# Half of the second plain expert as a fourth kind of group, and token sums of two batches made during attention

## The chip, the cores and the metric

The kernel runs on one core of one Trainium2 chip. The time is device microseconds of that core: 1470.93 us, the median of three runs (1470.7 to 1470.96).

## The reference

A gated linear attention is followed by a mixture of experts.

```
state = 0                                   # per batch (4) and head (8): 48 x 48
for t in range(768):
    state = f[t, :, None] * state + outer(k[t], v[t])      # f = sigmoid(f_logit)
    y[t] = q[t] @ state
x = y as (3072 tokens, 384 features)
P = exp(x @ w_gate - max)                   # 3072 x 8
8 times: P /= P.sum(1) + 1e-9; P /= P.sum(0) + 1e-9; P *= 3072 / 8
out = sum over e in 0..7 of P[:, e] * (relu(x @ w1[e]) @ w2[e])     # 384 -> 1024 -> 384
```

Every expert sees every token, so nearly all of the work is dense products.

## The kernel before

Each number is held as two fp16 parts (h and l), and a product is made of three: hh, hl, lh. The tokens are cut into 4 batches of 768; a batch is two units `u` of 384 tokens, a unit three tiles `t` of 128. The 1024 features of an expert are 8 tiles `f` of 128.

The program has three stages on the one core.

**Attention with plain experts as its filler.** There are 24 attention items, one for each 128 tokens. An item loads `q3` (decay, q, k) and `vr`, runs two scans on VectorE, makes fp16 parts on ScalarE and GpSimd, transposes by a DMA, and gives TensorE 24 products `aps`, 24 `kvps`, 48 `yps`, and 6 of the gate (`lps`). Its result is written into `xh` and `xl`, the two parts of the tokens. The code of an item is a generator. A loop over steps `g` advances each item that is alive by one `yield`; an item begins every 8 steps (`STEPS`), the fourth at step `LEADS`. In each step `fill(n)` adds so many TensorE products of the plain experts as the table `FILL` says for that step. The plain experts are 0 and 1 for all 8 units (`RAW`, 16 pairs of expert and unit): for a unit, 72 products `hps` (x by w1), then 72 `yps` (h by w2), all with 384 columns. The first three units (`TILED`) are done in tiles of 128 tokens, with `hps` products of 128 columns. After each `hps` bank ScalarE writes `hh`, the relu in fp16, and VectorE `hl`, what fp16 left out. A result `yr` goes to DRAM (`ys`) and is read back and scaled much later (`readds`).

**The balance.** After the last item the gate numbers `lg` of all tokens go through `sinkhorn`: eight rounds of small VectorE operations with one product `sk_c` each, which end in `pes`, the weight of each token and expert. Plain products go on as filler, 8 for a step. Beside them `convert` turns the tokens of a batch into the 15 sums that the third stage needs: `x32` (h + l), 17 sums `xs` on GpSimd, three maxima `xmx` on VectorE, then two fp16 parts of each (`xah`, `xal`, `xbh`, `xbl`), which take the place of `xh` and `xl`, so they come when no plain expert reads these tokens any more.

**Groups.** 48 groups (`ORDER`), one for each expert 2 to 7, half of its features (`m`, 512) and batch. A group makes the products with fewer multiplications: 15 block products for 18 with w1 (90 products of 256 columns), 7 for 8 with w2 in three blocks (126 products of 192 columns). The weights of a group are prepared some groups ahead (`prepare_w1`, `prepare_w2`). Before the first group, five products `kb_touch` mark the hand-over of the PSUM banks.

The order on each engine is fixed: `pin` chains each instruction behind the one before it on its engine, and `mm` does so on TensorE. Where the chain is cut (`last.clear()` before the groups), the scheduler may place an instruction earlier.

Of the kernel before, what the change touches and what calls it, by code (L numbers as in the profile page):

```python
# [50 lines left out]
RAW = [(e, u) for u in range(5) for e in range(2)] + [(0, 5), (0, 6), (0, 7), (1, 5), (1, 6), (1, 7)]  # L51
# [227 lines left out]
def fast(ctx, tc, qkf, vbd, wg, w1, w2, out, flag):  # L279
# [44 lines left out]
    psa = pctx.enter_context(tc.tile_pool(name="psa", bufs=2, space=PSUM))  # L324
# [60 lines left out]
    banks = [0]  # L385

    def bank(shape, name):
        n = banks[0]
        banks[0] += 1
        return (psn if n % 2 and not late else psm).tile(shape, F32, name=name, tag="m")  # L390

    def moe(e, u, w):
        w1s, w2s = w
# [3 lines left out]
        hh, hl = [], []  # L397
        for f in range(FT):
# [10 lines left out]
            th, tl = (hp.tile([128, 2, 256], F16, name=f"h{q}_{e}_{u}_{f}", tag=f"k{q}{f // 6}{f % 6 // 3}{f % 3}").rearrange("p c t -> p (c t)")[:, 0:HS] for q in "hl")  # L409
# [5 lines left out]
            yield 1  # L415
        for t in range(TT):
            ts = slice(t * 128, t * 128 + 128)
            ps = bank([128, DM], f"yps_{e}_{u}_{t}")
            n = 0
            for f in range(FT):  # L420
                wh, wl = w2s[f // 2]
                for a, b in ((hh[f], wh), (hh[f], wl), (hl[f], wh)):
                    mm(out=ps, lhsT=a[:, ts], rhs=b[:, f % 2, :], start=(n == 0), stop=(n == 3 * FT - 1))
                    n += 1
                    if n < 3 * FT:
                        yield 1
            with at(EPRIO):
                yr = rp.tile([128, DM], F32, name=f"yr_{e}_{u}_{t}", tag="yraw", bufs=3)
                pin(nc.scalar.activation(out=yr, in_=ps, func=AF.Copy))
                nc.sync.dma_start(out=yscr[e][u, t * 128:(t + 1) * 128], in_=yr)  # L430
            yield 1

    tiles, put_off, owed = [0], [False], []

    def moe_tile(e, u, t):
        w1s, w2s = ws[e]
# [4 lines left out]
        h = []  # L441
        for g in range(2):
# [24 lines left out]
            h.append([v.rearrange("p (f t) -> p f t", t=128) for v in (th, tl)])  # L467
            yield 1 / 3
        ps = bank([128, DM], f"yps_{e}_{u}_{t}")
        n = 0  # L470
        for f in range(FT):
            if len(owed) > 1 - f // 4:
                raise RuntimeError("a low part is owed")
            wh, wl = w2s[f // 2]
            hh, hl = (v[:, f % 4, :] for v in h[f // 4])
            for a, b in ((hh, wh), (hh, wl), (hl, wh)):
                mm(out=ps, lhsT=a, rhs=b[:, f % 2, :], start=(n == 0), stop=(n == 3 * FT - 1))
                n += 1
                if n < 3 * FT:
# [3 lines left out]
        nc.sync.dma_start(out=yscr[e][u, t * 128:(t + 1) * 128], in_=yr)  # L483
        yield 1
# [34 lines left out]
    def gate(i, xh, xl, tok):  # L519
        ps = psa.tile([128, 2 * NE], F32, name=f"lps{i}", tag="a", bufs=1)  # L520
# [18 lines left out]
    def early_item(i):  # L539
# [21 lines left out]
        r = ap.tile([R, L], F32, name=f"r_{i}", tag="r")  # L561
# [18 lines left out]
        qh = ap.tile([R, L], F16, name=f"qh_{i}", tag="qh")  # L580
        ql = ap.tile([R, L], F16, name=f"ql_{i}", tag="ql")
# [42 lines left out]
        aps = psa.tile([128, NB, C], F32, name=f"aps_{i}", tag="a", bufs=1)  # L624
# [23 lines left out]
        if i:  # L648
            kept = ap.tile([R, NP, D], F32, name=f"u1_{i}", tag="u1")
# [21 lines left out]
        yps = psa.tile([128, NP, TS], F32, name=f"yps_{i}", tag="y", bufs=1)  # L671
# [32 lines left out]
    def item(i):  # L704
# [15 lines left out]
        r = ap.tile([R, L], F32, name=f"r_{i}", tag="r")  # L720
# [21 lines left out]
        qh = ap.tile([R, L], F16, name=f"qh_{i}", tag="qh")  # L742
        ql = ap.tile([R, L], F16, name=f"ql_{i}", tag="ql")
# [10 lines left out]
        yield from wait(4)  # L754
# [7 lines left out]
        aps = psa.tile([128, NB, C], F32, name=f"aps_{i}", tag="a", bufs=1)  # L762
# [774 lines left out]
```

## Time and profile before

| | |
|---|---|
| median of three runs | 1470.93 us |
| the profiled execution | 1472.75 us |
| its span, first to last instruction | 1471.0 us |
| TensorE, share of the span with a matmul under way | 98% |
| VectorE / ScalarE / GpSimd busy | 82% / 74% / 72% |
| granted TensorE clock, mean | 0.995 |

The profile is of one execution; the difference of 1.75 us between its time and its span lies outside the instructions. An instruction that is still under way counts as busy, also while the next one of its engine has begun; so the busy time of a stretch is less than the sum of the durations in it. In the 40 slices of the page a digit is a busy share in tenths.

### The profile page before, as it was taken

The numbers are of one execution on the slowest core, as the hardware profiler recorded it, in microseconds if no ns is written. First come the engines' busy times: TensorE is split into PE (matmuls) and PEld (weight loads), VectorE is DVE, ScalarE is ACT, GpSimd is POOL, SyncE is SP. The second block draws the span as 40 slices with busy tenths as digits, with TensorE's granted clock in tenths as the row PEclk, the third lists the DMA queues.
The fourth block names the chain that finished last, engine by engine and source line by source line (L and its number), as shares of the span: only waits on it lengthen the run. The fifth ranks groups of instructions, "written<-read, shape, count | busy, mean of one in ns | idle before, by whom it ended". The sixth has DMA issues, their size and how long they took to land.

```text
span 1471.0 us, 40358 instructions
## 1 busy us (share of the span) xinstructions
PE 1445.4 (98%) x16051; PEld 1258.1 (86%) x16051; DVE 1208.6 (82%) x2494; ACT 1085.2 (74%) x2428; POOL 1062.2 (72%) x1242
## 2 busy tenths in 40 slices
PE   7899999999999999999999999999999999999997
PEld 5688886666666799999999999999999999999996
DVE  8767677775685799889998988888898989888776
ACT  7767777774343777888888888888877777778764
POOL 3244544555458566999999999999998888888763
PEclk9999999999999999999999999999999999999999
DMA  8345445441001101222111111111111101000012
GB/s 263 110 114 123 111 125 127 122 109 41 17 33 39 44 13 29 61 62 62 55 53 54 54 55 40 50 50 55 49 34 34 34 26 31 13 21 14 2 55 79
DMA packets 82807, 90.51 MB, mean 62 GB/s; under 512 B 49872, under 2 KB 69456, under 8 KB 82608
## 3 DMA queue, kind: packets, MB, share of 16 engines
q1 hardware_dynamic: 82176, 87.25, 21.3%
q8 instruction: 127, 2.08, 0.6%
q14 instruction: 72, 0.59, 0.1%
q10 hardware_dynamic: 432, 0.59, 0.1%
HBM read 64.03 MB, written 14.16 MB: 53 GB/s over the span
## 4 chain that ended last, share of the span: by engine, by line
PE 90%; DVE 5%; ACT 3%; DMA 1%; issue 1%; POOL 0%; DVEq 0%; ACTq 0%
PE kyps L307 28%; PE yps L307 14%; PE hps L307 11%; PE kb_A L307 8%; PE kb_B L307 8%; PE kb_D L307 6%; PE kxps L307 5%; PE kb_C L307 4%; PE kb_E L307 2%; PE kb_F L307 2%; PE aps L307 1%; PE kvps L307 1%; DMA w1r<-in_w_dram 0%; DVE w2l L380 0%; DVE acc L1242 0%
## 5 line engine op out<-in xcount | busy, mean ns | idle before, releaser
L307 PEld LDWEIGHTS <-k1h 128*128 128x128 f16 x2880 | 270.9, 98 | 22.4 <-issue 3.5
L307 PE MATMUL kyps<-k2h,kgh 128*128 128x192 f16 x1152 | 283.4, 246 | 1.5 <-ACT kyps L1239 1.5
L307 PE MATMUL kyps<-k2l,kgh 128*128 128x192 f16 x1152 | 283.4, 246 | 0.0
L307 PE MATMUL kyps<-k2h,kgl 128*128 128x192 f16 x1152 | 283.4, 246 | 0.0
L307 PEld LDWEIGHTS <-kgh 128*128 128x128 f16 x2304 | 212.1, 98 | 8.2 <-issue 1.8
L1412 POOL TENSOR_TENSOR kgl<-kf,kgh 128x512 f16<-128x512 f32 x141 | 186.7, 1324 | 2.8 <-ACT kgh L1409 2.8
L1242 DVE SCALAR_TENSOR_TENSOR yy<-kyps,pes,part 128x192 f32<-128x192 f32 x258 | 106.9, 415 | 89.8 <-PE kyps L307 78.9
L1412 POOL TENSOR_TENSOR kgl<-kr,kgh 128x512 f16<-128x512 f32 x141 | 167.2, 1186 | 9.5 <-PE kyps L307 8.1
L1281 POOL TENSOR_TENSOR acc<-acc,yy 128x384 f32<-128x384 f32 x129 | 129.1, 1001 | 61.4 <-DVE yy L1242 61.4
L307 PEld LDWEIGHTS <-k1l 128*128 128x128 f16 x1440 | 140.9, 98 | 16.3
L307 PE MATMUL yps<-w2h,hh 128*128 128x384 f16 x384 | 126.6, 330 | 1.9 <-ACT hh L458 1.8
L307 PE MATMUL yps<-w2h,hl 128*128 128x384 f16 x384 | 126.5, 329 | 1.2 <-DVE hl L461 1.2
L307 PE MATMUL yps<-w2l,hh 128*128 128x384 f16 x384 | 126.5, 329 | 0.4 <-DVE w2l L380 0.3
L307 PEld LDWEIGHTS <-w1h 128*128 128x128 f16 x1344 | 97.3, 98 | 33.4 <-issue 2.1
L307 PEld LDWEIGHTS <-hh 128*128 128x128 f16 x768 | 74.7, 99 | 47.8 <-ACT hh L458 2.4
L307 PEld LDWEIGHTS <-kh 128*128 128x128 f16 x1152 | 108.2, 98 | 8.1 <-issue 1.8
L307 PEld LDWEIGHTS <-kgl 128*128 128x128 f16 x1152 | 112.7, 98 | 0.2 <-issue 0.2
L1363 ACT ACTIVATE cp<-kb_A 128x512 f32<-128x512 f32 x144 | 86.1, 598 | 20.0 <-DVE kb_A L1365 16.3
L1239 ACT ACTIVATE kyps<-kyps 128x192 f32<-128x192 f32 x144 | 46.3, 322 | 66.0 <-PE kyps L307 63.3
L1409 ACT ACTIVATE kgh<-kf 128x512 f16<-128x512 f32 x144 | 91.0, 632 | 0.9 <-DVE kf L1386 0.6
L1409 ACT ACTIVATE kgh<-kr 128x512 f16<-128x512 f32 x144 | 90.4, 628 | 0.0
L1389 POOL TENSOR_TENSOR kr<-kr 128x256 f32<-128x256 f32 x96 | 72.9, 759 | 22.1 <-ACT kr L1378 20.1
(310 smaller groups left out, 5282.0 us busy)
## 6 DMA issues: line engine op xcount, KB each, us to landing
q<-in_qkf_dram SPq DMA_DIRECT2D x23, 672.0 KB, 5.3
k1r<-in_w_dram SPq DMA_DIRECT2D x24, 384.0 KB, 3.0
ys<-yr SPq DMA_DIRECT2D x48, 192.0 KB, 2.2
k2r<-in_w_dram SPq DMA_DIRECT2D x24, 384.0 KB, 3.1
yb<-ys SPq DMA_DIRECT2D x48, 192.0 KB, 2.4
vr<-in_vbd_dram SPq DMA_DIRECT2D x24, 192.0 KB, 2.5
out_dram<-acc SPq DMA_DIRECT2D x21, 192.0 KB, 1.9
w1r<-in_w_dram SPq DMA_DIRECT2D x8, 384.0 KB, 8.7
```

What stands on the lines that cost most here:

```text
L307: ins = (nc.tensor.transpose if transpose else nc.tensor.matmul)(**kw)
L1239: pin(nc.scalar.activation(out=out, in_=in_, func=AF.Copy, **kw))
L1242: pin(nc.vector.scalar_tensor_tensor(out=y, in0=ps, scalar=p, in1=z, op0=ALU.mult, op1=ALU.add))
L1281: pin(nc.gpsimd.tensor_tensor(out=y, in0=y, in1=z.rearrange("p s d -> p (s d)"), op=ALU.add))
L1363: pin(nc.scalar.activation(out=fresh(ev[2]), in_=bk, func=AF.Copy))
L1389: pin((nc.gpsimd if ev[2] == 'P' else nc.vector).tensor_tensor(out=r[:, 0], in0=r[:, 1], in1=r[:, 0], op=ALU.subtract))
L1409: pin(nc.scalar.activation(out=hs['g', t][0][i], in_=hs['f' if i else 'r', t], func=AF.Copy))
L1412: pin((nc.vector if tag == str(PERIODS - 1) else nc.gpsimd).tensor_tensor(out=hs['g', t][1][i], in0=hs['f' if i else 'r', t], in1=hs['g', ...
```

## The change

1. `FEATS` gives expert 1 only its first 4 feature tiles as a plain expert. Its other 512 features become four groups, (1, 1, b) for the four batches, at the head of `ORDER`, which now has 52 groups. Expert 1 loads four plain weight tiles for eight.
2. `RAW` goes through the pairs by unit; only the last pair is left over to the end of the filler (`RAW_END`), before three were.
3. Plain pairs are cut in an up part (w1) and a down part (w2), and the up part of what comes next is put ahead of a down part: always for the tiles, and one feature tile of the next pair for expert 1.
4. The converts of batches 0 and 1 run during attention (`EARLY`: from step 60 and from step 150, one `yield` in four steps). The other two begin at steps 1 and 30 of the balance, before at 26 and 50 (and the last at 67); the first group weights at step 13, before 34.
5. `LEADS` is 17 for 23, and `FILL` drops from 8.7, 8.1 a step to 5.6, 6.4 and 6.9.
6. An attention item has nine more waits (`MIDDLE` 6, `LATER` 2, one `yield`); the gate comes 6 steps behind x, before 4. From item 6 on, the fourth block of the tokens is written as one 96 x 128 piece `x3` on ScalarE and one on VectorE (before, three 32 x 128 pieces on each), and six DMAs on SP's queue move them to their partitions.
7. Some buffers of an item go from two to one, `qh` and `ql` to three, and the two `kvps` of an item share one PSUM bank, of which there is one (before two).
8. Tables of due steps for the weights of the groups (`W1AT0`, `W2AT0`, `W2AT1`, `W2AT3`, `CONVAT`) and for the plain weights of expert 1 (`SECONDAT`) are written anew.

Counted in the program: 324 `hps` products of 128 columns, 180 of 384, and 288 `yps` of 384 go away; 4 x 216 products of groups are added. 108 DMAs of x3 are added.

```diff
-RAW = [(e, u) for u in range(5) for e in range(2)] + [(0, 5), (0, 6), (0, 7), (1, 5), (1, 6), (1, 7)]
+FEATS = (FT, FT // 2)
+RAW = [(e, u) for u in range(3) for e in range(2)] + [(0, 3), (1, 3), (0, 4), (1, 4), (0, 5), (1, 5), (0, 6), (1, 6), (0, 7), (1, 7)]
+RAW_END = 1
...
-ORDER = [(e, m, b) for e in range(2, NE) for m in range(2) for b in range(B)]
+ORDER = [(e, m, b) for e in range(1, NE) for m in range(2) if (e, m) != (1, 0) for b in range(B)]
...
-LEADS = 23
-FILL = (... (17, 5.3), (23, 8.7), (30, 8.7), (43, 8.1), (48, 8.1))
+LEADS = 17
+FILL = (... (17, 5.3), (23, 5.6), (48, 6.4), (112, 6.9), (160, 6.9))
...
-CONVSTEP = (26, 50, 67)
-KSTEP = 34
+CONVSTEP = (1, 30)
+KSTEP = 13
+EARLY = ((60, 4, 30), (150, 4, 13))
...
+        if i >= X3_FROM:
+            x3 = ap.tile([96, 2, TS], F16, name=f"x3_{i}", tag="x3", bufs=1)
+            pin(nc.scalar.activation(out=x3[:, 0, :], in_=yps[0:96, 3], func=AF.Copy, scale=YS * XS))
...
+            pin(nc.vector.scalar_tensor_tensor(out=x3[:, 1, :], in0=yps[0:96, 3], scalar=YS * XS, in1=x3[:, 0, :], op0=ALU.mult, op1=ALU.subtract))
...
+            for q, x in enumerate((xh, xl)):
+                for n in range(3):
+                    nc.sync.dma_start(out=x[96:128, n, tok], in_=x3[32 * n:32 * n + 32, q, :])
...
+        for e, u, t in todo:
+            h = []
+            yield from tile_up(e, u, t, h)
+            behind_.append((e, u, t, h))
+            while len(behind_) > (0 if e == u == 0 and t < TT - 1 or (e, u, t) == (1, 0, TT - 1) or u and e else 1):
+                yield from tile_down(*behind_.pop(0))
...
+            yield from moe_up(*p, h)
+            if p[0] and n + 1 < len(todo):
+                first_up[todo[n + 1]] = ([], [])
+                yield from moe_up(*todo[n + 1], first_up[todo[n + 1]], 1)
+            yield from moe_down(*p, h)
...
+        for b, (begin_, every, most) in enumerate(EARLY):
+            if begin_ <= g < begin_ + every * most and (g - begin_) % every == 0:
+                next(converts[b], None)
```

Two places in the order of VectorE bear on the prediction. The first is in the first 70 us. `w2l` is the low part of a plain weight tile, `k2r` the raw tile of weights of the first group, whose transfer can begin only when `w2l` has freed a buffer; `wmx` reads it. Before:

```order
L380 SCALAR_TENSOR_TENSOR w2l_2_1163<-w2r_2_709,w2h_2_1162 128x768
L732 SCALAR_TENSOR_TENSOR q_3_1019<-q_3_1019,r_1129 112x512
L733 SCALAR_TENSOR_TENSOR vlc_1134<-vr_1021,vhc_1133 128x384
L734 SCALAR_TENSOR_TENSOR q_3_1019<-ft_129,pi_130 112x512
L380 SCALAR_TENSOR_TENSOR w2l_3_1167<-w2r_3_725,w2h_3_1166 128x768
L1096 TENSOR_REDUCE wmx<-k2r_0_8525 128x1
L461 SCALAR_TENSOR_TENSOR hl_0_0_0_1250<-hps_0_0_0_1211,hh_0_0_0_1249 128x512
```

And now:

```order
L397 SCALAR_TENSOR_TENSOR w2l_3_556<-w2r_3_186,w2h_3_555 128x768
L640 TENSOR_TENSOR carry_715<-kvps_586,st_576 112x192
L601 SCALAR_TENSOR_TENSOR q_2_494<-ft_129,pi_130 112x512
L723 SCALAR_TENSOR_TENSOR xl_318<-yps_641,xh_317 96x3x128
L723 SCALAR_TENSOR_TENSOR xl_318<-yps_641,xh_317 32x128 x3
L607 TENSOR_TENSOR q_2_494<-q_2_494 112x512
L555 TENSOR_REDUCE lg<-lps_732 128x8
L647 TENSOR_TENSOR kb_128<-q_2_494,kb_128 48x8x64 x2
L1158 TENSOR_REDUCE wmx<-k2r_2_7605 128x1
L661 SCALAR_TENSOR_TENSOR vlc_748<-vr_496,vhc_747 128x384
```

`wmx` stood straight behind the `w2l` that frees the buffer; now nine instructions stand between, and it is one item earlier.

The second place is the end of the balance, ahead of `kb_A`, the first VectorE work of the groups. Before, these rows stand ahead of it, and `pes` 36 rows ahead:

```order
L412 SCALAR_TENSOR_TENSOR hl_7_5_8385<-hps_7_5_8370,hh_7_5_8384 128x384
L1024 TENSOR_REDUCE xmx<-x_3_8296 128x1
L412 SCALAR_TENSOR_TENSOR hl_7_6_8402<-hps_7_6_8388,hh_7_6_8401 128x384
L412 SCALAR_TENSOR_TENSOR hl_7_7_8420<-hps_7_7_8405,hh_7_7_8419 128x384
L1024 TENSOR_REDUCE xmx<-x_3_8296 128x1
L1365 TENSOR_TENSOR kb_A<-kb_A,cp_13_8552 128x512
```

And now:

```order
L168 TENSOR_SCALAR sk_cs<-sk_c_7520 128x8
L169 RECIPROCAL sk_cs<-sk_cs 128x8
L170 TENSOR_SCALAR sk_cs<-sk_cs 128x8
L172 TENSOR_TENSOR pe<-pe,sk_cs 128x192
L1113 TENSOR_SCALAR pes<-pe 128x192
L1418 TENSOR_TENSOR kb_A<-kb_A,cp_13_7624 128x512
```

The last round of the balance now stands directly ahead of the groups. On TensorE, 396 products stand between the last gate product and the first `kb_touch`, before 682.

## Rows read from the trace of the kernel before

**Rows 1.** The page: busy time of each engine, and the chain of work that ended last by engine.

```profile
PE 1445.4 (98%) x16051; PEld 1258.1 (86%) x16051; DVE 1208.6 (82%) x2494; ACT 1085.2 (74%) x2428; POOL 1062.2 (72%) x1242
...
PE 90%; DVE 5%; ACT 3%; DMA 1%; issue 1%; POOL 0%; DVEq 0%; ACTq 0%
```

**Rows 2.** Busy time by stretch (start:end, length, then busy us and count of each engine, granted clock, DMA share, GB/s). The stretches are cut where items 1, 2, 3, 6 and 22 give TensorE their `yps`, and by the stages.

```profile
33.59:50.94 17.35, 15.01 (x225) 11.45 (x222) 14.63 (x25) 11.45 (x23) 4.02 (x6) 1.00 0.45 137
50.94:89.05 38.11, 35.56 (x492) 28.25 (x490) 25.55 (x43) 25.64 (x51) 12.83 (x13) 0.96 0.43 113
89.05:130.81 41.76, 41.45 (x700) 34.36 (x698) 29.75 (x58) 29.95 (x65) 19.52 (x20) 1.00 0.50 117
130.81:345.62 214.81, 214.59 (x3019) 159.34 (x3017) 160.84 (x322) 158.62 (x343) 106.05 (x110) 1.00 0.46 113
...
530.00:1440.00 910.00, 909.81 (x9717) 863.62 (x9716) 800.30 (x1688) 728.65 (x1674) 787.17 (x913) 1.00 0.14 41
```

**Rows 3.** The chain of waits, its longest pieces (start, us, engine, output, line, count). The first is `hps` of 128 columns, the next two are `yps` of two attention items that follow each other, then `hps` and `yps` of 384 columns.

```profile
96.21 4.02 PE hps L307 x72
...
305.50 1.40 PE yps L307 x48
...
318.93 1.40 PE yps L307 x48
...
436.32 11.70 PE hps L307 x72
448.02 11.70 PE yps L307 x72
```

**Rows 4.** The timeline of VectorE about 69 us (start, us; in brackets the idle time before and what ended it).

```profile
64.63 0.93 DVE L380 SCALAR_TENSOR_TENSOR w2l<-w2r,w2h 128x768 f16<-128x768 f32 x1
68.96 0.95 DVE L1096 TENSOR_REDUCE wmx<-k2r 128x1 f32<-128x768 f32 x1 [3.40 <-DMA k2r<-in_w_dram]
69.83 1.28 DVE L461 SCALAR_TENSOR_TENSOR hl<-hps,hh 128x512 f16<-128x512 f32 x2
```

**Rows 5.** The timeline of TensorE there.

```profile
69.35 0.34 PE L307 MATMUL yps<-w2h,hh 128*128 128x384 f16 x1 [1.83 <-ACT hh L458]
...
70.57 0.50 PE L307 MATMUL yps<-w2h,hl 128*128 128x384 f16 x1 [0.72 <-DVE hl L461]
70.86 0.53 PE L307 MATMUL yps<-w2h,hh 128*128 128x384 f16 x1
71.18 0.53 PE L307 MATMUL yps<-w2l,hh 128*128 128x384 f16 x1
...
73.74 0.44 PE L307 MATMUL yps<-w2h,hh 128*128 128x384 f16 x1
```

**Rows 6.** Busy time in the ten microseconds of that place, as in rows 2.

```profile
70.00:80.00 10.00, 9.43 (x115) 6.90 (x116) 5.69 (x10) 5.42 (x12) 3.40 (x6) 0.83 0.62 162
```

**Rows 7.** Groups of instructions by form (line, engine, operation, output and inputs, shapes, count; busy us, mean ns of one; idle before). VectorE, ScalarE and GpSimd.

```profile
L412 DVE SCALAR_TENSOR_TENSOR hl<-hps,hh 128x384 f16<-128x384 f32 x80 | 43.9, 550 | 51.9 <-ACT hh L411 51.4
L821 DVE SCALAR_TENSOR_TENSOR xl<-yps,xh 32x128 f16<-32x128 f32 x63 | 18.1, 287 | 0.9
L615 DVE TENSOR_TENSOR kb<-q,kb 48x512 f16<-48x512 f32 x6 | 5.1, 850 | 0.1
L573 DVE TENSOR_TENSOR_SCAN q<-ft,pi 112x512 f32<-112x512 f32 x3 | 3.7, 1217 | 0.0
L1043 DVE TENSOR_TENSOR xal<-xs,xah 128x768 f16<-128x768 f32 x12 | 13.0, 1092 | 0.1
L1024 DVE TENSOR_REDUCE xmx<-x 128x1 f32<-128x768 f32 x12 | 11.2, 937 | 0.0
L1043 DVE TENSOR_TENSOR xbl<-xs,xbh 128x512 f16<-128x512 f32 x8 | 6.3, 803 | 0.0
...
L411 ACT ACTIVATE hh<-hps 128x384 f16<-128x384 f32 x80 | 39.1, 489 | 43.3 <-PE hps L307 39.7 <-DVE sk_rs L151 1.0 <-DVE xmx L1024 1.0
L429 ACT ACTIVATE yr<-yps 128x384 f32<-128x384 f32 x30 | 14.7, 490 | 54.4 <-PE yps L307 36.6 <-issue 17.7
L818 ACT ACTIVATE xh<-yps 32x128 f16<-32x128 f32 x63 | 16.8, 266 | 1.0
L818 ACT ACTIVATE xh<-yps 96x384 f16<-96x384 f32 x21 | 10.1, 481 | 10.6 <-PE yps L307 10.6
...
L1021 POOL TENSOR_TENSOR xs<-x 128x256 f32<-128x256 f32 x40 | 30.8, 785 | 23.4 <-DVE sk_cs L160 15.2 <-DVE xmx L1024 5.0 <-DVE x L1007 3.0
L1007 POOL TENSOR_TENSOR x<-xh,xl 128x768 f32<-128x768 f16 x9 | 15.1, 1710 | 0.0
```

**Rows 8.** DMA issues of the page (KB each, us to landing).

```profile
ys<-yr SPq DMA_DIRECT2D x48, 192.0 KB, 2.2
```

**Rows 9.** The timeline of VectorE at the last gate number and at the end of the balance, and then of TensorE at the first product of the groups and of ScalarE at the first use of `pes`.

```profile
369.99 0.16 DVE L527 TENSOR_REDUCE lg<-lps 128x8 f32<-128x16 f32 x1
...
435.20 0.51 DVE L1051 TENSOR_SCALAR pes<-pe 128x192 f32<-128x192 f32 x1
...
480.87 0.27 PE L307 MATMUL kb_A<-xbh,k1h 128*128 128x256 f16 x1
...
503.35 0.41 ACT L1239 ACTIVATE part<-kyps,pes 128x192 f32<-128x192 f32 x1
```

**Rows 10.** Busy time by stretch, as in rows 2, between the last gate number and the first group.

```profile
370.00:481.00 111.00, 110.59 (x690) 67.24 (x688) 75.97 (x155) 45.08 (x92) 67.32 (x85) 1.00 0.09 30
```

More of the change, by code (lines that the diff above doesn't have):

```diff
@@ L389, in bank, with moe_up @@
         banks[0] += 1
-        return (psn if n % 2 and not late else psm).tile(shape, F32, name=name, tag="m")
-    def moe(e, u, w):
-        w1s, w2s = w
+        return (psn if n % 2 and not (late or final[0]) else psm).tile(shape, F32, name=name, tag="m")
+    tiles, put_off, owed = [0], [False], []
+    def moe_up(e, u, h, to=FT):
+        w1s, (hh, hl) = ws[e][0], h
         if not all((u, t) in ready for t in range(TT)):
@@ L396, in moe @@
         xh, xl = xof(u)
-        hh, hl = [], []
-        for f in range(FT):
+        for f in range(len(hh), min(to, FEATS[e])):
             wh, wl = w1s[f // 2]
@@ L440, in moe_tile @@
         ts = slice(t * 128, t * 128 + 128)
-        h = []
-        for g in range(2):
+        for g in range(FEATS[e] // 4):
             ps = bank([128, 4, 128], f"hps_{e}_{u}_{t}_{g}")
@@ L483, in moe_tile @@
         nc.sync.dma_start(out=yscr[e][u, t * 128:(t + 1) * 128], in_=yr)
+        if t == TT - 1:
+            over.add((e, u))
         yield 1
@@ L803, in item @@
         yield
+        yield from wait(LATER)
         if not s:
@@ L930, in fast, with left @@
+    over = set()
+    def left(b):
+        return lambda: sum(p[1] // 2 == b and p not in over for p in RAW)
+    converts = [convert(b, left(b)) for b in range(B)]
     fixed[0] = True
@@ L945, in fast @@
     first = [load(0, 1 + n // 4, n % 4) for n in range(8)]
-    second = [load(1, 1 + n // 4, n % 4) for n in range(8)]
+    second = [load(1, 1 + n // 2, n % 2) for n in range(4)]
     wgen = gate_weights()
@@ L974, in fast @@
         at_steps(first[n], *FIRSTAT[n - 2])
-    for n in range(8):
+    for n in range(4):
         at_steps(second[n], 4 + n, *SECONDAT[n])
@@ L1126, in first_maxima @@
             for k in (1, 2):
-                for j in range(4):
+                for j in range(FEATS[e] // 2):
                     raw = raw_weights(e, k, j, "m").rearrange("p a f -> p (a f)")
@@ L1158, in fast @@
     chain = balance()
-    converts = [convert(b, left(b)) for b in range(B)]
-    work = [converts[0]]
-    kw = None
+    work = [converts[0], converts[1]]
+    kw, closed = ctx.enter_context(tc.tile_pool(name="kw", bufs=4, reuse_waits="tile")), False
     step, held_mm = 0, None
@@ L1167, in fast @@
         more = fill(LEAD * 3 / 8)
-        if not more and kw is None:
+        if not more and not closed:
+            closed = True
             wctx0.close()
-            kw = ctx.enter_context(tc.tile_pool(name="kw", bufs=4, reuse_waits="tile"))
             filler = raws()
@@ L1180, in fast @@
         if step in CONVSTEP:
-            work.append(converts[1 + CONVSTEP.index(step)])
+            work.append(converts[2 + CONVSTEP.index(step)])
         if step == KSTEP:
-            work.append(chained(prepare_w1(ORDER[0][0], j, (5,)) for j in range(2)))
+            work.append(chained(prepare_w1(ORDER[0][0], 2 * ORDER[0][1] + j, (5,)) for j in range(2)))
     while True:
```

260 lines of the change are left out of this document (139 added, 121 removed).

## The prediction

> **What bounds the kernel now.** I read the page's busy shares and the chain of waits first. TensorE has a matmul under way for 98% of the span and makes up 90% of the chain [rows 1], so the first question is how much TensorE work the change takes away, and the second whether TensorE stays the engine that is waited for. A busy share of the whole span can't answer the second, so I then cut the span into stages [rows 2]. From 89 us on TensorE is busy for all but 0.5 of 256 us of attention, and for all but 0.2 of 910 us of groups. Beside it VectorE is busy 75% of the attention stretch (160.84 of 214.81 us) but 88% of the groups (800.30 of 910), GpSimd 49% and 87%. The only long stretch that loses time lies ahead, between items 2 and 3 (50.94 to 89.05 us), where TensorE lacks 2.6 us and the clock is at 0.96. So a TensorE product that goes is worth its full spacing, as long as the other engines keep up.
>
> **Products removed and added.** The spacing comes from the chain: 72 products of 384 columns take 11.70 us, or 162.5 ns each, and 72 of 128 columns 4.02 us, or 55.8 ns [rows 3]. Removed are 324 x 55.8 ns = 18.1 us and 468 x 162.5 ns = 76.1 us, 94.1 us together. In the groups, 9717 products fill 910 us [rows 2], 93.65 ns each; a group has 216, which is 20.23 us, and four are 80.9 us. Net -13.2 us. The four groups stand at the head of the same sequence, with the same work beside them, so this price carries over. Their weights, readds and maxima ride in the periods as the others' do.
>
> One rule of the Trainium skill speaks against this exchange of wide products for narrow ones. The page "TensorE: Matmul & The Clock Gate", section "Back-to-back issue gap", says that in a stream of weight loads and matmuls both set the spacing: 81 ns at 128 columns, 131 ns at 512. On a line between them, as an estimate, 384 columns would cost 114 ns, 256 columns 98 and 192 columns 87; 79.6 us would go and 79.1 come. The trace disagrees at both shapes that go, 162.5 and 55.8 ns [rows 3].
>
> **The first 90 us.** VectorE waits 3.40 us for the raw weights of the first group [rows 4], since the transfer starts only when `w2l` has freed the buffer and `wmx` stands right behind. Behind it wait the two `hl`, and TensorE waits for those: 1.83 and 0.72 us idle [rows 5]. The products that follow, from 70.57 to 73.74 us, come 0.32 us apart, the 1.2 GHz level, and the granted clock of those ten us is 0.83 [rows 6]; ten products at 0.32 for 0.1625 lose 1.6 us more. Together 4.1 us. In the changed order a scan (1.22 us), two `kb` (0.85 each), three small `xl` (0.29 each) and more stand between: at least 3.8 us [rows 7], more than the wait of 3.40. So this stall can go. What is late next is the rest of the start: item 3 begins six steps sooner, so the filler between items 2 and 3 is less while VectorE has nearly the same items to feed, and from item 1 to item 2 it is busy 14.63 of 17.35 us already [rows 2]. Four fewer plain weight tiles relieve it. Bounds -4.1 and +3; I take -2, half of the stall.
>
> **Attention.** Two items follow each other in 13.43 us [rows 3], where `FILL` is 8.1: 8 x 8.1 x 0.1625 = 10.53 us of filler and 2.9 us of the item. With 5.6, 6.4 and 6.9 an item takes 10.2, 11.2 and 11.9 us of TensorE. Nothing is lost by that alone; the filler that isn't done here is done later. But the other engines have less time for an item. In the stretch of 16 items VectorE needs 10.05 us an item, ScalarE 9.91, GpSimd 6.63 [rows 2]. At 6.4 there are 2.2 us of filler less, and a plain pair of 23.4 us costs VectorE eight `hl` of 0.550 us and ScalarE eight `hh` of 0.489 and three `yr` of 0.490 [rows 7]: -0.42 and -0.51 us. The x3 piece replaces three by one. Its shape, 96 x 128, isn't in the trace; on ScalarE it lies between 0.266 (32 x 128) and 0.481 (96 x 384), and I take 0.266, because the columns are the same; on VectorE 0.287. That saves 0.53 and 0.57 us. The early convert of batch 0 adds three `xmx`, three `xal` and two `xbl`, 7.7 us of VectorE over ten items, and 17 sums of 0.785 and three of 1.71 on GpSimd, 18.5 us over some seven [rows 7]. So VectorE comes to 9.8 of 11.2 us (88%), GpSimd to 9.3 (83%), ScalarE to about 9.4 (84%); in the three items at 5.6, without x3, VectorE to 9.4 of 10.2 (93%). That is what the groups show without loss [rows 2], save for those three items. The added waits give each item nine more steps between its links, so a link that is 1 us late has cover. The six DMAs of x3 wait in SP's queue for ScalarE and VectorE, and behind them stand the next item's loads and its transpose; a small transfer lands in 2.2 us [rows 8], and the gate stands six steps (8 us) behind. I price them at nothing; if a tile is still not there when an expert reads it, TensorE stands. Bounds 0 and +21 (1 us an item); I take +2, for the three tight items and their neighbours.
>
> **The balance.** Between the last gate product and the hand-over there were 682 products, now 396, or 64.4 us. The rounds from the last gate number to `pes` took 65.7 us (369.99 to 435.71), and `pes` was first used 22.5 us behind the first product of the groups [rows 9]. So the 45 us of cover are gone, and `pes` ends about as the groups begin, with 21 us still to spare. VectorE's load: its rows between those two places, each by its mean duration, sum to 83.3 us before, where the trace shows 75.97 busy [rows 10]; now the same sum is 64.1, so 58 us of 64.4 (91%). A round of the balance with most of the converts in it is over-full for some us. Bounds 0 and +10; I take +1.
>
> **Sum.** -13.2 - 2 + 2 + 1 = -12.2 us. Against the profiled execution, 1472.75 us (span 1471.0), that is 1460.5; the median of the runs is 1.8 us below that execution, so I expect 1470.93 - 12.2 = 1458.7 us.
>
> **Rivals.**
> Attention becomes the bound of VectorE and ScalarE: their fixed order makes an `hh` or `hl` stand behind an item's instruction that waits for GpSimd or a DMA, and TensorE runs dry. For it: 93% in three items, and one wait of 3.4 us on VectorE cost TensorE 4.1 [rows 4 to 6]. Against it: the groups run at 88% without loss. It decides from 14.2 us, 0.68 us an item over 21 items; at 1 us an item the time is 1477.7. 11%.
> The balance loses its cover: VectorE falls behind in the rounds, and each `sk_c` waits in TensorE's row; 10 us late gives 1467.7. For it: 91% load in a chain of small dependent operations. Against it: 21 us before `pes` is needed. 10%.
> More is won: the stall at 69 us goes in full, nothing is lost in attention or balance, and the start's other idle time shrinks: 1453.6 and less. 9%.
> The exchange buys nothing, because at the head of the sequence a group costs not 20.2 us but 94.1 / 4 = 23.5 us (109 ns a product): 1471.9 with the other three terms at +1, no change. Against it: 9717 products of groups in a row at 93.65 ns [rows 2]. The skill's rule above leads to about the same time. 2%.
> The forecast, 1454 to 1465: 68%.
>
> **How the numbers follow.** A measurement of this kernel tells 0.2% (2.9 us) from no change, so faster means under 1468.0. The forecast and the third rival lie there, and of the second rival six parts in ten; the first gives half that on a smaller loss: 0.68 + 0.09 + 0.06 + 0.03 = 0.86. Slower takes most of the rest of the first rival, 0.08; within the bound 0.06. The range of 8 in 10 goes from 1451 (all of 4.1, and 2 us of the start) to 1470, through the second rival and the mild part of the first. The likeliest case's own range is 1454 to 1465.
>
> **What would show it.** The groups should start some 95 us sooner than 481 and a group still take 20.2 us; if it takes longer, the price of the exchange is wrong. Item 3 should come at about 78 us for 89. From there to the last item TensorE's idle time should stay under 4 us; idle time that ends in an `hh`, `hl` or `ql` over 10 us speaks for the first rival, one that ends in `sk_cs` or `pes` for the second. A wait of VectorE on `k2r` as long as before would disprove the start. The prediction is wrong if TensorE lacks more than 10 us in sum from 60 us to the groups.

## The result, and the profile after

The changed kernel takes 1492.32 us (median of four runs, 1488.95 to 1493.33), the kernel before 1470.95 beside it: a ratio of 1.0141, 95% interval [1.0124, 1.0159]. It is 21 us slower, where 12 us faster was forecast. The page of its profiled execution (1491.82 us, span 1490.1), to set beside [rows 1]:

```profile
PE 1442.1 (97%) x16123; PEld 1273.9 (85%) x16123; DVE 1283.2 (86%) x2567; ACT 1117.1 (75%) x2505; POOL 1147.3 (77%) x1322
...
PE 75%; DVE 11%; ACT 4%; issue 4%; POOL 3%; DMA 3%; SPq 0%; DVEq 0%; POOLq 0%; ACTq 0%
```

TensorE's part of the chain fell from 90 to 75%, VectorE's rose from 5 to 11%. To see where, cut the span at places that both kernels have: the output product of items 3 and 23, the first `kb_touch` product (there the work passes to the groups), the groups. First two stretches of the kernel before, then three of the changed one (columns as in [rows 2]):

```profile
89.00:359.00 270.00, 269.47 (x3884) 202.96 (x3882) 197.95 (x391) 193.24 (x417) 130.47 (x134) 1.00 0.44 109
359.00:479.10 120.10, 120.10 (x795) 73.82 (x793) 79.35 (x163) 48.32 (x100) 78.24 (x99) 1.00 0.09 31
```

```profile
79.20:335.00 255.80, 238.08 (x3453) 175.75 (x3451) 222.96 (x353) 178.81 (x382) 175.32 (x171) 0.99 0.50 121
335.00:415.30 80.30, 76.38 (x520) 46.05 (x516) 62.18 (x133) 33.79 (x70) 45.63 (x61) 1.00 0.11 38
500.00:1400.00 900.00, 899.93 (x9615) 854.42 (x9613) 794.95 (x1661) 727.69 (x1670) 793.31 (x922) 1.00 0.13 38
```

In the 20 items from 3 to 23 TensorE idles 17.7 us, for 0.5 before. With each product at the price of its shape, in the order of the program, the products of that stretch make 230.6 us (270.7 before), so it lost 25.2 us (before -0.7); the stretch behind it holds 74.9 us of products (120.2 before) and lost 5.4 (before -0.1). The groups run as before: 9615 products in 900 us, 93.6 ns each. The account: removed products -94.1, start -1.1 (item 3 at 79.2 us with 55.3 us of products ahead of it, before 89.0 with 64.0), attention +25.9, balance +5.5, groups +82.9 (from the hand-over at 415.3 to the end 1074.8 us, before 991.9), in sum +19.1, the difference of the two spans.

What TensorE waited for in that stretch of attention (engine and line, what it waited for: us, times, longest):

```profile
PE yps L315 <- DVE sl L835: 7.5, 7, 1.8
PE hps L315 <- DMA xl<-x: 2.3, 1, 2.3
PE yps L315 <- DVE hl L484: 2.2, 6, 0.6
PE yps L315 <- ACT hh L481: 1.7, 3, 1.1
```

It is VectorE that is late, above all with `sl`, and VectorE is busy 87% of the stretch. The forecast had 9.8 us of it an item; 222.96 us over 20 items are 11.1. What grew are single instructions. Durations of one line (count: least, median, most in ns; first and last start), before:

```profile
L721 DVE TENSOR_TENSOR_SCAN r<-ft,ind x21: 1214/1224/1226, 59.4 to 330.7; 112x512 f32<-112x512 f32 x21
...
L801 DVE SCALAR_TENSOR_TENSOR sl<-st,sh x42: 340/556/1882, 84.7 to 357.3; 48x384 f16<-48x384 f32 x36, 48x192 f16<-48x192 f32 x6
```

and after:

```profile
L753 DVE TENSOR_TENSOR_SCAN r<-ft,ind x21: 1202/1271/3877, 50.7 to 305.8; 112x512 f32<-112x512 f32 x21
...
L755 DVE TENSOR_SCALAR pi<-r x21: 174/176/2318, 52.0 to 307.7; 112x8 f32<-112x8 f32 x21
...
L835 DVE SCALAR_TENSOR_TENSOR sl<-st,sh x42: 323/984/2928, 78.3 to 331.6; 48x384 f16<-48x384 f32 x36, 48x192 f16<-48x192 f32 x6
...
L811 DVE SCALAR_TENSOR_TENSOR am<-aps,mask x21: 674/682/692, 69.1 to 322.7; 128x512 f32<-128x512 f32 x21
```

The same scan takes up to 3.9 us, an instruction of 8 columns up to 2.3; `am`, which reads PSUM, keeps its 0.68. The timelines of VectorE and then of GpSimd at one such place (start, us):

```profile
127.77 3.64 DVE L835 SCALAR_TENSOR_TENSOR sl<-st,sh 48x384 f16<-48x384 f32 x2
```

```profile
127.35 1.26 POOL L769 TENSOR_TENSOR q<-q 112x512 f32<-112x512 f32 x1 [2.35 <-DVE q L766]
128.57 1.63 POOL L991 TENSOR_TENSOR x<-xh,xl 128x768 f32<-128x768 f16 x1
130.17 0.82 POOL L790 TENSOR_TENSOR st<-carry,tds 112x192 f32<-112x192 f32 x1
```

Two `sl` that take 1.11 us elsewhere take 3.64 beside GpSimd's `q` and the early `x`. Comparing all starts and ends from 50 to 345 us: 40 of the 42 `sl` now lie beside a GpSimd instruction and are 0.67 us longer than the shortest on the mean (before 17 of 40, 0.35); the two others 0.03. 14 of the 21 `r` do, none before. The 21 `am` all do, and are 0.01 longer. The `sl` and `r` that are longer by 0.1 us or more end a fixed time behind the end of a GpSimd instruction: 22 `sl` of 384 columns after 0.41 to 0.42 us, three of 192 after 0.22, nine `r` after 1.08 to 1.11. They wait for it, and only then work.

### The profile page after: what moved, and what is told of

Same layout as the page of the kernel before. It is cut to its first block, busy times and chain, and to the rows that moved or that the text cites. A ratio compares the mean times of both kernels' runs of the same rounds, so it can differ in the third digit from the quotient of the medians.

```text
span 1490.1 us, 40995 instructions
## 1 busy us (share of the span) xinstructions
PE 1442.1 (97%) x16123; PEld 1273.9 (85%) x16123; DVE 1283.2 (86%) x2567; ACT 1117.1 (75%) x2505; POOL 1147.3 (77%) x1322
## 4 chain that ended last, share of the span: by engine, by line
PE 75%; DVE 11%; ACT 4%; issue 4%; POOL 3%; DMA 3%; SPq 0%; DVEq 0%; POOLq 0%; ACTq 0%
PE kyps L315 30%; PE kb_B L315 9%; PE kb_A L315 9%; PE kb_D L315 7%; PE kxps L315 5%; PE kb_C L315 4%; PE hps L315 3%; PE yps L315 3%; PE kb_E L315 2%; PE kb_F L315 2%; DVE r L753 2%; DVE sl L835 1%; POOL xs L1004 1%; DMA q<-in_qkf_dram 1%; DVE q L766 1%
## 5 line engine op out<-in xcount | busy, mean ns | idle before, releaser
L315 PEld LDWEIGHTS <-k1h 128*128 128x128 f16 x3120 | 293.5, 98 | 26.0 <-issue 5.6
L315 PE MATMUL kyps<-k2h,kgh 128*128 128x192 f16 x1248 | 307.0, 246 | 1.5 <-ACT kyps L1292 1.5
L315 PE MATMUL kyps<-k2h,kgl 128*128 128x192 f16 x1248 | 307.0, 246 | 0.0
L315 PE MATMUL kyps<-k2l,kgh 128*128 128x192 f16 x1248 | 307.0, 246 | 0.0
L1465 POOL TENSOR_TENSOR kgl<-kf,kgh 128x512 f16<-128x512 f32 x153 | 206.5, 1350 | 2.7 <-ACT kgh L1462 2.7
L315 PEld LDWEIGHTS <-k1l 128*128 128x128 f16 x1560 | 152.6, 98 | 17.7
L315 PEld LDWEIGHTS <-w1h 128*128 128x128 f16 x1008 | 74.7, 99 | 32.9 <-issue 11.0
L315 PE MATMUL yps<-w2h,hl 128*128 128x384 f16 x288 | 94.1, 327 | 2.9 <-DVE hl L484 2.2
L315 PE MATMUL yps<-w2h,hh 128*128 128x384 f16 x288 | 94.2, 327 | 1.8 <-ACT hh L481 1.7
L315 PE MATMUL yps<-w2l,hh 128*128 128x384 f16 x288 | 94.1, 327 | 1.1 <-DVE w2l L397 1.1
L1292 ACT ACTIVATE kxps<-kyps 128x192 f32<-128x192 f32 x156 | 49.4, 317 | 51.9 <-PE kyps L315 45.6
```

The costliest lines, as they stand in the source:

```text
L315: ins = (nc.tensor.transpose if transpose else nc.tensor.matmul)(**kw)
L1292: pin(nc.scalar.activation(out=out, in_=in_, func=AF.Copy, **kw))
L1465: pin((nc.vector if tag == str(PERIODS - 1) else nc.gpsimd).tensor_tensor(out=hs['g', t][1][i], in0=hs['f' if i else 'r', t], in1=hs['g', ...
```

## The experiments

The changed kernel stands behind all edits unless the kernel before is named. Ratios are to the kernel before, with their interval.

**Theory 1: the early sums lengthen VectorE's instructions, and that is the loss.** Four runs, and the rivals: too little filler for an item (2), or GpSimd's queue (3).

```diff
-EARLY = ((60, 4, 30), (150, 4, 13))
-CONVSTEP = (1, 30)
+EARLY = ()
+CONVSTEP = (12, 22, 30)
```

> Theory 1 (GpSimd's token sums stretch VectorE's instructions whose operands all lie in SBUF: r, pi, st, sl): without early sums the scan r goes back to 1.2 us at most 1.4, sl to a mean under 0.8 us, and the output product of item 23 comes at 308 to 318 us for 335. Theory 2 (an item has too few steps of filler, whatever GpSimd does): item 23 stays at 330 or later. The whole is no test: four converts now lie in the balance, so 1475 to 1500 us by either.

Measured: 1496.4 us, 1.0168 [1.0151, 1.0185]. Attention (item 3 to 23), then the rest up to the groups:

```profile
77.40:318.80 241.40, 233.09 (x3452) 173.93 (x3450) 195.58 (x342) 173.66 (x373) 132.94 (x131) 1.00 0.54 128
318.80:415.70 96.90, 81.39 (x520) 47.73 (x517) 75.11 (x144) 38.20 (x79) 78.31 (x95) 0.94 0.09 32
```

Item 23 comes 16 us sooner, at 318.8, just past the late end of what theory 1 said; but `r` still reached 2.4 us, `sl` took 0.99 us on the mean, and 10.8 us are lost against the products (230.6), so not all goes with the sums. The 14.4 us won between the two items are given back: the balance takes 96.9 us for 80.3, and the hand-over stays at 415.7.

```diff
-            pin(nc.gpsimd.tensor_tensor(out=block(r), in0=block(p), in1=block(q), op=ALU.add if op == '+' else ALU.subtract))
+            pin((nc.vector if b < 2 else nc.gpsimd).tensor_tensor(out=block(r), in0=block(p), in1=block(q), op=ALU.add if op == '+' else ALU.subtract))
```

> The 17 sums and the three x32 of batches 0 and 1 on VectorE: some 17 x 0.35 + 3 x 0.8 = 8.4 us more of VectorE for each batch, and 18 us less of GpSimd. Theory 1: the stretching (45 us more than before over the attention) goes, which is more than the 17 us added; item 23 at 318 to 327 us, the whole 1474 to 1484. Theory 2, VectorE is merely over-full: 17 us more work on it makes item 23 later, 340 to 350, the whole 1497 to 1507.

1492.48 us, 1.0137 [1.0120, 1.0154]: item 23 at 334.7, nothing won, nothing lost. VectorE is busy 232 us of the 257 from item 3. Neither theory's number came. `sl` and `r` together took 69.3 us for 83.7, so there was less waiting, and more work in its place.

The next run leaves the sums of these two batches out; GpSimd writes constants in their place, three times each.

```diff
-            pin(nc.gpsimd.tensor_tensor(out=block(r), in0=block(p), in1=block(q), op=ALU.add if op == '+' else ALU.subtract))
+            if b < 2:
+                for _ in range(3):
+                    pin(nc.gpsimd.memset(block(r), 1.0))
+            else:
+                pin(nc.gpsimd.tensor_tensor(out=block(r), in0=block(p), in1=block(q), op=ALU.add if op == '+' else ALU.subtract))
```

> Leaves out the 17 token sums of batches 0 and 1: GpSimd writes constants there, three times each, so that it is busy about as long but reads nothing. Theory 1 (both engines reading SBUF collide): r at 1.2 us, item 23 at 312 to 322, the whole 1468 to 1480. Theory 3 (the sums stand in GpSimd's queue ahead of q, kb, ql and al, and that delay is what counts): VectorE's durations may go back but item 23 stays at 331 to 337 and the whole at 1488 to 1494. Theory 2: the same as theory 3.

1489.18 us, 1.0118 [1.0102, 1.0135], item 23 at 330.4: 3 us won, in the range of theories 2 and 3 (item 23 a little before it). One detail stands for the collision all the same: three `sl`, an `r` and two `st` that lay beside constants alone were at most 0.03 us longer than their shortest. The rest still met GpSimd's `q`, `ql` and `al`.

On the kernel before, 60 GpSimd additions are put into attention; `extra` is a scratch tile.

```diff
+        if 60 <= g < 180 and g % 4 == 0:
+            for _ in range(2):
+                pin(nc.gpsimd.tensor_tensor(out=extra[:, 2], in0=extra[:, 0], in1=extra[:, 1], op=ALU.add))
```

> The kernel before, with 60 more GpSimd additions of 128x256 in attention, two in every fourth step from step 60 to 180, the pace of the early converts; they add to a scratch tile. Theory 1: the mean of sl rises from 0.75 to 1.0 us or more, r's maximum from 1.23 to over 2 us; VectorE has a quarter of its time free there, so the time rises by 0 to 8 us only. Theory 2 and 3: durations as before, r at most 1.3 us, time within 2 us of before.

1474.92 us, 1.0022 [1.0013, 1.0032]. Item 3 to 23, and `r`:

```profile
87.30:360.70 273.40, 270.33 (x3883) 202.62 (x3881) 216.53 (x391) 192.17 (x417) 189.20 (x194) 1.00 0.42 108
```

```profile
L721 DVE TENSOR_TENSOR_SCAN r<-ft,ind x21: 1212/1431/1860, 59.5 to 333.5; 112x512 f32<-112x512 f32 x21
```

The same 391 instructions of VectorE take 18.6 us more (216.53 for 197.95): the lengthening is shown by itself. But under 13.5 us of TensorE's work an item it costs only 2.4 us.

**The order of the steps.** If what matters is which steps coincide, moving them should pay.

```diff
-MIDDLE = 6
-LATER = 2
+MIDDLE = 4
+LATER = 3
...
         yield
-        yield
         for (o, rs), (hi, _) in zip(sl, sh):
```

> Of the changed kernel, the links between an item's steps as before (four steps ahead of aps, sl one step behind carry), and three steps ahead of the output product for two; all else stays. sl then no longer falls in the step of GpSimd's q. Theory 1 in its second form (what counts is which VectorE step falls beside which GpSimd step): sl's mean falls from 1.14 to under 0.9 us, item 23 comes at 322 to 330 us for 335.0, the whole is 1478 to 1487. If the added steps were the cover that keeps attention going (theory 4), aps and the output product wait for kb, ql and al instead: item 23 later than 336, the whole over 1494.

1507.5 us, 1.0237 [1.0220, 1.0254]. VectorE's work in attention fell to 203 us, yet item 23 came at 348.4: TensorE now waits for the landing of `xl` (8.1 us) and of `kt` (5.9). Theory 4: the added steps are cover that the pace needs.

```diff
-EARLY = ((60, 4, 30), (150, 4, 13))
+EARLY = ((58, 8, 15), (146, 8, 7))
...
-                next(converts[b], None)
+                for _ in range(2):
+                    next(converts[b], None)
```

> As the run before, and the early sums in one step of eight, the one in which VectorE reads PSUM (am), four sums at a time. Theory 1, second form: VectorE's lengthening over 100 to 300 us falls from 48 us to under 20, item 23 at 312 to 322, the whole 1468 to 1478. If the place of the sums doesn't matter, only their number, it equals the run before within 3 us.

With both edits 1513.78 us, 1.0285 [1.0268, 1.0302]; with this one alone:

> The changed kernel with only the early sums moved to that one step of eight. Theory 1, second form: r and pi go back to 1.2 and 0.18 us, sl stays long (GpSimd's q is still beside it), item 23 at 325 to 331, the whole 1481 to 1488. If only their number matters: 1489 to 1494.

1497.86 us, 1.0177 [1.0160, 1.0194], `r` up to 5.1 us. Theory 1 in its second form falls: four sums in a row do more harm than two.

```diff
-X3_FROM = 6
+X3_FROM = 24
```

> The changed kernel with the three small copies in place of x3 and its six DMAs. VectorE and ScalarE get 0.57 and 0.53 us more for each of 18 items. If VectorE's load is what holds attention, item 23 comes 4 to 10 us later than 335.0 and the whole is 1496 to 1503. If x3's DMAs hold it (TensorE waited 3.6 us for them), 331 to 334, the whole 1486 to 1490.

1498.54 us, 1.0182 [1.0165, 1.0199], item 23 at 339.8: x3 is worth some 6 us. TensorE's waits that end in `sl` rise from 7.5 to 13.3 us, which speaks for VectorE's load, though ScalarE's rises too. The DMAs of x3, for whose landing TensorE waits 3.6 us in the changed kernel, cost less than x3 saves.

**How much is VectorE's load?** The next run leaves `sl` out (the state's low half stays zero).

```diff
-        for (o, rs), (hi, _) in zip(sl, sh):
-            pin(nc.vector.scalar_tensor_tensor(out=o, in0=sf[rs], scalar=SS, in1=hi, op0=ALU.mult, op1=ALU.subtract))
```

> The changed kernel without sl, the low half of the carried state (it stays zero): 41 us of VectorE's time go, 16 of work and 25 of waiting beside GpSimd. If VectorE's time, that waiting included, holds attention (theory 1): item 23 at 316 us or sooner for 335.0, the hand-over to the groups at 398 or sooner for 415.3, the whole 1475 or less. If the links from item to item hold it (theory 4), VectorE's load doesn't matter: item 23 at 328 or later, the whole 1485 or more.

1484.63 us, 1.0090 [1.0072, 1.0108].

```profile
77.80:325.90 248.10, 234.16 (x3453) 173.86 (x3452) 175.83 (x312) 178.18 (x382) 166.05 (x171) 0.99 0.52 124
```

47 us less of VectorE (175.83 for 222.96, now 71% busy) win 8 us, and TensorE still idles 13.9. Item 23 comes at 325.9, between theory 1 (316 or sooner) and theory 4 (328 or later): VectorE's load is a part of it, not the bound.

```diff
+        pin(nc.scalar.activation(out=sf, in_=sf, func=AF.Copy, scale=SS))
...
-            pin(nc.vector.scalar_tensor_tensor(out=o, in0=sf[rs], scalar=SS, in1=hi, op0=ALU.mult, op1=ALU.subtract))
+            pin(nc.gpsimd.tensor_tensor(out=o, in0=sf[rs], in1=hi, op=ALU.subtract))
```

> The changed kernel with sl on GpSimd, which can't wait for itself; ScalarE scales the state for it, one instruction more for an item. VectorE loses 41 us, GpSimd gains some 42 x 0.9 = 38, ScalarE 13. Theory 1: item 23 at 318 to 328, the whole 1476 to 1486. If GpSimd becomes the bound (11.8 us an item where it converts), 335 or later and 1492 or more.

1513.59 us, 1.0280 [1.0261, 1.0298]: the rival's number, though GpSimd is busy only 214 of 278 us. The edit also puts `carry` ahead of the new instruction; ScalarE waits 12.9 us for it (from 89 to 340 us), and TensorE 15.6 us for `hh`. So the run says little of theory 1.

**The pace alone.** The kernel before, nothing removed, with the filler of the changed one:

```diff
-FILL = ((0, 11.7), (1, 10.3), (2, 0), (3, 0), (5, 2), (6, 0), (7, 6), (8, 6), (9, 0), (10, 6), (12, 5.3), (15, 5.3), (17, 5.3), (23, 8.7), (30, 8.7), (43, 8.1), (48, 8.1))
+FILL = ((0, 11.7), (1, 10.3), (2, 0), (3, 0), (5, 2), (6, 0), (7, 6), (8, 6), (9, 0), (10, 6), (12, 5.3), (15, 5.3), (17, 5.3), (23, 8.7), (30, 5.6), (54, 6.4), (118, 6.9), (166, 6.9))
```

> The kernel before with the changed kernel's filler in attention (5.6, 6.4, 6.9 products a step for 8.7 and 8.1), nothing removed: the products not done there are done in the balance, which has later steps for its converts. The prediction's claim that less filler costs nothing by itself: items 10.2 to 11.9 us apart, the time 1469 to 1475. If the other engines and the links can't follow at that pace even with the old order and without early sums (theory 4): items 12.3 us or more apart, TensorE idle for 15 us or more, the time 1483 or more.

1496.0 us, 1.0167 [1.0149, 1.0186]. It is 23.6 us slower than the kernel before, without a product removed, an early sum or a new order in an item. In the profiled execution 17.8 us are there at the hand-over (496.9 for 479.1), and 3.8 come behind it, for which nothing was tried. The changed kernel, with 94.1 us of products less, has lost 30.3 us at its hand-over (415.3 + 94.1 - 479.1), so less filler alone comes to more than half of that. Then 7.5 and 6.0 products a step throughout: `(30, 7.5)` and `(30, 6.0)` as the last pair of the table. In all three the balance is longer, and its converts and first weights have later steps.

> The kernel before with 7.5 products of filler a step in attention from step 30 on, an item of 12.65 us of TensorE. If the other engines need a fixed time for an item in this order (some 12 us, as the run with less filler showed where it had 6.9), nothing is lost here: items 12.6 to 12.8 us apart, TensorE idle under 3 us, the time 1469 to 1477. If any filler taken away is lost in proportion (half of what goes): 1477 to 1481.

> The same with 6.0 products a step, an item of 10.7 us of TensorE. With a floor near 12 us for an item, items come 11.9 to 12.7 us apart whatever the filler, and 20 items lose some 24 to 40 us of TensorE: the time 1495 to 1513. If only the first tight stretch (5.6) lost, as it may seem from the run before: under 1490.

1485.32 us, 1.0091 [1.0074, 1.0108], and 1520.27, 1.0334 [1.0317, 1.0352], both longer than was expected. Item 3 to 23 of the three, with 5.6 to 6.9, 7.5 and 6.0 products:

```profile
83.00:329.10 246.10, 234.41 (x3684) 179.55 (x3683) 198.74 (x380) 184.70 (x402) 129.92 (x133) 1.00 0.48 118
```

```profile
86.50:339.20 252.70, 252.70 (x3811) 194.32 (x3809) 191.19 (x383) 188.06 (x409) 130.06 (x133) 1.00 0.46 116
```

```profile
84.10:340.90 256.80, 225.89 (x3590) 170.28 (x3589) 199.44 (x371) 181.68 (x393) 126.99 (x132) 0.99 0.45 110
```

With 5.6 to 6.9 products TensorE idles 11.7 us in that stretch, for 17.7 in the changed kernel and 0.5 before. At 7.5 an item takes the 12.63 us that TensorE needs, without idle time (the run's loss lies in the balance, where its moved steps make one wait of 9.4 us). At 6.0 it takes 12.84 us on the mean for 10.7: a fifth less filler than 7.5, and items no faster. VectorE is busy 78%, ScalarE 71% and GpSimd 49%: no engine is full. But this is no fixed floor for an item. The mean is of two paces, to item 16 and behind it:

```profile
84.10:259.00 174.90, 149.77 (x2552) 117.26 (x2551) 135.23 (x243) 121.92 (x261) 83.85 (x89) 0.99 0.47 117
259.00:340.90 81.90, 76.12 (x1040) 53.02 (x1039) 64.20 (x129) 59.76 (x133) 43.15 (x43) 1.00 0.41 96
```

In the first, where the filler is in tiles, 13 items come 13.45 us apart, hardly sooner than in the kernel before (13.6 there), and TensorE's waits end in `hh` (17.8 us) and `hl` (5.8). In the second, with products of 384 columns, seven items come 11.7 us apart. What holds the first pace: VectorE, ScalarE, GpSimd and TensorE about one item.

```profile
151.26 1.23 DVE L721 TENSOR_TENSOR_SCAN r<-ft,ind 112x512 f32<-112x512 f32 x1
...
153.88 1.22 DVE L734 TENSOR_TENSOR_SCAN q<-ft,pi 112x512 f32<-112x512 f32 x1
...
159.32 2.03 DVE L787 TENSOR_TENSOR st<-u,tds 112x192 f32<-112x192 f32 x1
...
165.11 1.23 DVE L721 TENSOR_TENSOR_SCAN r<-ft,ind 112x512 f32<-112x512 f32 x1
```

```profile
161.44 1.07 ACT L794 ACTIVATE sh<-st 48x384 f16<-48x384 f32 x2 [2.11 <-DVE st L787]
162.53 0.60 ACT L458 ACTIVATE hh<-hps 128x512 f16<-128x512 f32 x1
```

```profile
155.18 1.27 POOL L737 TENSOR_TENSOR q<-q 112x512 f32<-112x512 f32 x1 [2.34 <-PE kvps L307]
156.41 2.38 POOL L746 TENSOR_TENSOR kb<-q,kb 48x512 f16<-48x512 f32 x2
158.87 1.15 POOL L753 TENSOR_TENSOR ql<-q,qh 112x512 f16<-112x512 f32 x1
159.98 1.16 POOL L795 TENSOR_TENSOR al<-am,ah 128x512 f16<-128x512 f32 x1
```

```profile
163.18 0.34 PE L307 MATMUL yps<-w2h,hh 128*128 128x384 f16 x1 [1.77 <-ACT hh L458]
```

In these rows it is a ring. GpSimd's `q` starts as VectorE's second scan ends, at 155.1 us (this row names `kvps`; in the kernel before the same wait ends in that scan); `kb`, `ql` and `al` follow in a row to 161.1; `st`, 0.35 us where it lies alone, takes 2.03 beside `ql` and `al`; ScalarE's `sh` waits for it, `hh` stands behind `sh`, TensorE waits for `hh`, VectorE's `hl` and `sl` behind that, and then comes the next item's `r`, 13.85 us after the last. In that run `st` has a median of 2.03 us. The reading is that a shorter step brings the instructions of two items closer in each fixed row, and that they wait round the ring; the next run was to test it.

Whether the added links of the changed kernel break the ring was tried on the kernel before, with that filler:

```diff
-        yield from wait(4)
+        yield from wait(6)
         st = ap.tile([R, CT, NP, D], F32, name=f"st_{i}", tag="st")
...
+        yield
         for (o, rs), (hi, _) in zip(sl, sh):
...
+        yield from wait(2)
         if not s:
...
-        yield from wait(4)
+        yield from wait(6)
         yield from gate(i, xh, xl, tok)
```

> The kernel before with the changed kernel's filler (as in the run that gave 1496) and the changed kernel's added steps between the links. If the links were what was late at that pace, the added steps win back most of the 24 us: 1473 to 1482. If it is the engines' work in their fixed order: 1490 to 1500.

1559.48 us, 1.0596 [1.0569, 1.0623], and nothing is learned of it: the gate's product there shares a PSUM bank with `aps`, and TensorE waits 35.2 us for `am` to free it.

**Can the idle time be filled?** More of the filler into attention, less into the balance:

```diff
-FILL = ((0, 11.7), (1, 10.3), (2, 0), (3, 0), (5, 2), (6, 0), (7, 6), (8, 6), (9, 0), (10, 6), (12, 5.3), (17, 5.3), (23, 5.6), (48, 6.4), (112, 6.9), (160, 6.9))
-LEAD = 8
+FILL = ((0, 11.7), (1, 10.3), (2, 0), (3, 0), (5, 2), (6, 0), (7, 6), (8, 6), (9, 0), (10, 6), (12, 5.3), (17, 5.3), (23, 5.6), (48, 6.4), (112, 7.9), (160, 7.9))
+LEAD = 5.5
```

> The changed kernel with 7.9 products of filler a step for 6.9 from step 112 (item 15) on, where its tokens allow it, and 5.5 products for 8 in each step of the balance. If TensorE's idle time in attention is time that the other engines need anyway (a floor for an item), the filler goes in for nothing: items 15 to 23 at 13.2 us as their products ask, TensorE without idle time there, the hand-over 6 to 12 us sooner than 415.3, the whole 1479 to 1487. If the balance and its converts need their 65 to 70 us whatever TensorE does: hand-over at 418 to 424, the whole 1494 to 1500.

1506.18 us, 1.0240 [1.0223, 1.0257]. With 7.4 and 6.5, 1494.09, 1.0159 [1.0142, 1.0176]:

> Half of that: 7.4 products in attention from step 112 on, 6.5 in the balance. By the floor: hand-over 3 to 7 us sooner, 1484 to 1490; by the balance's own need: 1491 to 1496.

With 7.4 and 8 a step, and the last convert at step 24 for 30, 1496.35 us, 1.0168 [1.0152, 1.0185]:

> 7.4 products in attention from step 112 on and 8 in the balance as it was, so that its last rounds have no filler left. The end of the filler comes before pes: hand-over 0 to 6 us sooner than 415.3 by the floor, with the last rounds open, 1486 to 1493; by the balance's own need at 418 or later, 1494 or more.

Attention and the rest up to the groups with 7.9, and TensorE's wait in that rest:

```profile
77.50:344.00 266.50, 250.66 (x3539) 183.68 (x3537) 228.19 (x358) 183.36 (x391) 174.75 (x171) 0.99 0.51 118
344.00:426.50 82.50, 67.00 (x433) 39.24 (x430) 62.14 (x128) 29.37 (x62) 45.71 (x61) 0.94 0.09 30
```

```profile
PE sk_c L315 <- DVE sk_cs L164: 15.5, 8, 5.2
```

The added filler hardly goes into the idle time: TensorE still idles 15.8 us in attention, for 17.7, and item 23 comes 9 us later. The balance takes its 80 us with 67 of TensorE's work as with 76, so nothing is won there. No version here beats the kernel before.

## Why the prediction was wrong

**The exchange (-13.2) was right**: the groups run at 93.6 ns a product, and the four more cost 82.9 us for 80.9.

**The start (-2) was right**: -1.1, item 3 at 79.2 us for about 78; the wait for `k2r` is gone (ten instructions stand ahead of `wmx`, not nine), VectorE's waits there end in `hh`.

**Attention (+2) is the step that failed**, at +25.9, by the sentence "Nothing is lost by that alone; the filler that isn't done here is done later." In the old kernel, less filler alone left TensorE idle for 11.7 us in that stretch and brought the hand-over 17.8 us late. The forecast compared each engine's work with the item's time and found 88% enough because the groups run at that share. But an item's instructions wait for each other round the fixed orders: at 6.0 products a step, 13 items came 13.45 us apart with no engine full. On top of this the early sums cost 14.4 us in attention, or 16.6 in the balance when they were moved there. The second fault is in VectorE's 9.8 us: durations of the old order, carried into one where `sl` and `r` lie beside GpSimd. They came to 11.1; `sl` is 0.39 us longer, twice an item, and `r` 0.5, about the difference (`st` and `pi` are longer too, by 0.22 and 0.27). ScalarE (8.9) and GpSimd (8.8) came out below the 9.4 and 9.3; the terms that the prediction shows for ScalarE make 8.9. The DMAs of x3, priced at nothing, made TensorE wait 3.6 us.

**The balance (+1)** lost 5.5: TensorE waits 3.6 us for `sk_cs`, the second rival at about half its price. Its cover was right, `pes` wasn't what was late; the rounds were.

**The first rival** (the fixed order) was it in kind, at 1.3 us an item for 1.0 and 11% of chance, but not by its own sign: 6.1 us of TensorE's idle time in attention end in `hh` or `hl`, where the sign was over 10, and 7.5 end in `sl`. Its chance was too low: the trace had 13.4 us as the only pace ever shown. The sign of being wrong, over 10 us of TensorE's time, came with 17.7 in attention alone.

One slip changes nothing in the sum: on the line that the prediction draws between two figures of the Trainium skill ("TensorE: Matmul & The Clock Gate", section "Back-to-back issue gap"), 192 columns make 89 ns, not 87, and so 80.2 us would come by that estimate, not 79.1.

How the loss splits isn't settled. Less filler cost 17.8 us at the hand-over in the old kernel and the early sums 14.4 us of attention in the changed one, against 30.3 in all; but the two were measured in different orders, and they overlap (the ring's `st` is itself lengthened beside GpSimd). The ring was read in the old kernel at 6.0 products alone. In the changed kernel without early sums TensorE idles 8.3 us in attention, and its waits end in the landing of x3 (3.7 us), `hl` (2.0) and `hh` (1.6): that the same ring holds its items isn't shown. More filler from the first items on wasn't tried there: its experts would be ahead of their tokens.

## What to carry to other kernels

Filler on the bounding engine is also the time that the other engines have. Before taking it away, run the old kernel with only the filler reduced, at two or three levels: that shows the pace at which items really come (here no idle time at 7.5 products a step, 11.7 us of it at 5.6 to 6.9), which busy shares don't show where the engines wait for each other in fixed orders. Durations hold only beside the same neighbours: where VectorE and GpSimd both read SBUF, a moved step changes them.

## What the runs showed of the hardware

A VectorE instruction whose operands all lie in SBUF (`r`, `pi`, `st`, `sl`) can wait inside its recorded duration for GpSimd, even for several of its instructions in a row: one `pi` took 2.3 us for 0.17, until `ql` and two `xs` behind it were done, and the profile counts that as busy time of VectorE. All six `pi` that waited ended 0.03 to 0.04 us behind the end of a GpSimd instruction. The 21 `am`, which read PSUM, didn't wait, nor did the `sl`, `r` and `st` beside GpSimd's constants (0.03 us at most). It goes the other way too: `al`, 1.16 us, took up to 2.11, beside an `r`.

The Trainium skill ("SBUF — State Buffer", section "SBUF: two separate sides") says that the two engines share a pair of ports, that the one that starts first has it for its whole instruction, and that the other is blocked until then. The runs agree where an instruction waited: its end follows the other engine's by its own work.
